# Attention, soft MoE and a squared-ReLU layer on one core: the start of the kernel rearranged around its branch

## The chip, the cores and the metric

The kernel runs as one program on one core of one Trainium2 chip. The metric is the device time of an execution in microseconds (us), and where several executions are given, their median. The engines are named as in the profile: PE is TensorE (PEld its weight loads), ACT is ScalarE, DVE is VectorE, POOL is GpSimd, SP is SyncE, which here only issues DMAs. A q behind an engine's name is its sequencer, which handles branches, waits and DMA issues.

## What is computed

Three layers in a row, all in float32. The sizes are 4 batches of 448 tokens, 12 heads of 64 (so 768 wide, and 24 pairs of heads over the batches).

```python
scores = matmul(q, k.T) / sqrt(64)
scores = cap * tanh(scores / cap)
attn = softmax(scores);  x = attn @ v                    # (4*448, 768)
logits = x @ phi                                         # phi: (768, 32)
d = softmax(logits, over tokens);  slot_input = d.T @ x  # 32 slots, 4 for each of 8 experts
slot_out[e] = relu(slot_input[e] @ w1[e]) @ w2[e]        # w1 (768, 1024), w2 (1024, 768)
x = softmax(logits, over slots) @ slot_out
h = relu(x @ w_in);  out = (h * h) @ w_out               # w_in (768, 2048), w_out (2048, 768)
```

## The kernel before

The order of all instructions is written out by hand (`manual_schedule`), so each engine executes its own instructions in the order of the code and waits on semaphores for the others.

*The start* (lines 76 to 245). SP requests `cap`. DVE makes `cabs` and `flag` of it; `flag` tells whether the cap is small enough for a softmax without its maximum. POOL meanwhile writes constants: one element of each ring buffer, the identity `ident`, `onesp` (for the sums of the softmax), `gcol`, `one1`, and then the selectors: `seld` and `selh` are sums of slices of `ident`, `ssum` and `selr` their copies spread over more columns. `ssum` sums over the four groups of tokens at the very end of attention (`last_end`), `selr` spreads the reciprocal sums of the last two pairs over the heads (`den_rows`, tile `bm`). Last, POOL clears `ktail` and `vtail`, which hold the last 64 rows of keys and values of a pair.

*Around the branch* (lines 576 to 586). SP requests the q and k of pairs 0 and 1 (`load`, tile `r`) and `phi` in four pieces. Then every engine reads `flag` into a register and branches for itself; there is no barrier. The block for a large flag stands first in the program, and the one that is executed here is reached by a jump. In it POOL requests the v of pair 0 (`load_v`, six pieces `va` and two `vtail`), DVE splits q and k into `hi` and `lo` (two parts whose products need one pass each), and SP requests pair 2 into the buffer of pair 0, for which it waits until `lo` has been made.

*A pair of heads* (`for i in range(NPAIR)`, 24 iterations). PE makes the scores in four groups of keys (`scores(i, g)`): three groups of 128 (line 323, two heads side by side) and the last 64 of both heads together (line 318, which reads `ktail`), each as three terms of `hi` and `lo`. There are two buffers for the scores, and ACT frees one with the tanh of a group (lines 327 and 325); ACT also makes the exponentials, two groups at a time (line 333). Between the groups of pair i, PE makes the products of pair i-1 with its v (`pv`, float32), the sums of its softmax (`den`, tile `dn`) and, from the fourth iteration on, the logits of pair i-3 with `phi_sb`. A float32 product is recorded twice, so six `pv` products are twelve records. DVE makes `hi` and `lo` of the next pair, and POOL fills `ktail` and requests v. SP's queue holds, in the order of the code, the q and k three pairs ahead, the spread of the reciprocal sums (`bc`), and the experts' weights.

*After attention* the experts run as fast as their weights come (lines 860 and 885), and then the last layer (lines 969 and 1089), where PE is never idle for long.

Of the kernel before, what the change touches and what calls it, by code (L numbers as in the profile page):

```python
# [8 lines left out]
F32 = mybir.dt.float32  # L9
# [10 lines left out]
P = 128  # L20
# [22 lines left out]
def softcap_attention_soft_moe_relu2(  # L43
# [75 lines left out]
    one1 = tmp.tile([1, 1], F32, name="one1")  # L119
    nc.gpsimd.memset(one1, 1.0)  # L120
    seld = tmp.tile([P, NS], F32, name="seld")
    add = lambda out, a, b: nc.gpsimd.tensor_tensor(out=out, in0=a, in1=b, op=ALU.add)
    ids = ident.rearrange("p (j s) -> p j s", j=4)
    add(seld, ids[:, 0], ids[:, 1])
    for j in (2, 3):
        add(seld, seld, ids[:, j])
    ssum = tmp.tile([P, 4, NS], F32, name="ssum")
    nc.gpsimd.tensor_copy(ssum, seld.unsqueeze(1).to_broadcast([P, 4, NS]))

    selh = tmp.tile([P, 2], F32, name="selh")  # L130
    idh = ident.rearrange("p (c h x) -> p c h x", c=4, h=2)[:, :, :, 0]
    add(selh, idh[:, 0], idh[:, 1])
    for c in (2, 3):
        add(selh, selh, idh[:, c])
    selr = tmp.tile([P, 2, D], F32, name="selr")
    nc.gpsimd.tensor_copy(selr, selh.unsqueeze(2).to_broadcast([P, 2, D]))
    phi_sb = tmp.tile([P, KD, NS], F32, name="phi_sb")


# [90 lines left out]
    with ExitStack() as att:  # L230
# [34 lines left out]
        def load(i):  # L265
            b, two, h = heads_of(i)
            t = raw_tile(i)
            nc.sync.dma_start(out=t, in_=qk[b, two, :, :, h].rearrange("j d r s -> (j d) r s"))
            st["raw", i] = t
# [59 lines left out]
        def exps(i, half):  # L329
            p = st["p", i, half].rearrange("p c h s -> p (c h s)")  # L330
            if half:
                p = p[:, :3 * S]
            nc.scalar.activation(p, p, AF.Exp, scale=cabs)  # L333
# [239 lines left out]
            if steps:  # L573
                steps.pop(0)()

        for i in range(2):
            load(i)
        for j in range(2):
            for h in range(2):
                nc.sync.dma_start(out=phi_sb[D * j:D * j + D, h::2], in_=phi[D * h:D * h + D, j::2])  # L580
        flag_v = nc.values_load(flag[:1, :1], min_val=0, max_val=1)
        with tc.If(flag_v == 0, preferred_fallthrough_block=False) as cond:
            load_v(0)
            prep_hi(0)
            prep_lo(0)
            load(2)
            for i in range(NPAIR):
                last = i == NPAIR - 1
                prv, old, tok = (i >= n for n in (1, 2, 3))
                scores(i, 0)  # L590
                scores(i, 1)
                exps(i, 0)
                if old:
                    take(i - 2)
                if tok:
                    norm(i - 3)
                if prv:
                    sums(i - 1, 1)
                if old:
                    den_rows(i - 2)  # L600
                if not last:
                    prep_hi(i + 1)
                    prep_lo(i + 1)
                if i + 3 < NPAIR:
                    load(i + 3)
                if prv:
                    for g in range(NG):
                        pv(i - 1, g)
                    den(i - 1, i - 3 if tok else None)
                if tok:  # L610
                    logits_add(i - 3)
                    if (i - 3) % HP == HP - 1:
                        late = batch_end((i - 3) // HP)
                        late.pop(0)()
                    elif (i - 3) % HP in (1, 2):
                        step()
                if i in range(4, 16, 2):
                    load_weight(NPAIR // 2 - 1 + (i - 4) // 4, part=i // 2 % 2)
                if i == NPAIR - 2:
                    load_weight(NB - 2, part=0)  # L620
                    load_weight(NB - 2, part=1)
                if (i, 2) in dsteps:
                    dsteps.pop((i, 2))()
                if i < 2 * len(early) and i % 2 == 0:
                    x = early[i // 2]
                    load_raw(*x, ring[NB - 1 - i // 2 % 2][:, :WSZ])
                    dsteps[i + 1, 1] = lambda x=x: decode_a(x)
                    dsteps[i + 2, 0] = lambda x=x: decode_b(x, nc.vector)
                    dsteps[i + 2, 1] = lambda x=x: decode_c([x], (0, 1))
                    dsteps[i + 3, 0] = lambda x=x: decode_c([x], (2,))  # L630
                    dsteps[i + 4, 2] = lambda x=x: store(x)
                if i % 2 and i < NPAIR - 1:
                    load_weight(i // 2)
                if (i, 0) in dsteps:
                    dsteps.pop((i, 0))()
                scores(i, 2)
                scores(i, 3)
                exps(i, 1)
                if prv:
                    pv(i - 1, NG)  # L640
                sums(i, 0)
                if tok:
                    to_tokens(i - 3)
                    if (i - 3) % HP == 0:
                        step()
                if not last:
                    load_v(i + 1)
                if i == 2:
                    load_weight(NB + 1)
                if i == NPAIR - 2:  # L650
                    load_weight(NB)
                    load_weight(NB - 3, part=0)
                    load_weight(NB - 3, part=1)
                if tok and (i - 3) % HP == HP - 1:
                    late.pop(0)()
                    steps.extend(late)
                if (i, 1) in dsteps:
                    dsteps.pop((i, 1))()
                if i == NPAIR - 4:
                    load_weight(NB - 1)  # L660
            assert not dsteps
            assert not steps
            n = NPAIR - 1
            pv(n, 0)
            pv(n, 1)
            sums(n, 1)
            den_rows(n - 1)
            load_weight(NB + 2, nc.scalar)
            pv(n, 2)
            pv(n, 3)  # L670
            norm(n - 2)
            norm(n - 1)
            den(n)
            to_tokens(n - 2, nc.scalar)
            logits(n - 2)
            den_rows(n)
            logits(n - 1, False)
            load_weight(NB + 3, nc.scalar)
            load_weight(NB + 4, nc.scalar)
            norm(n)  # L680
            to_tokens(n - 1, nc.scalar)
            logits(n, False)
            last_end(True)

        with cond.Else():
            st.clear()
            for n, x in enumerate(early):
                load_raw(*x, ring[NB - 1 - n % 2][:, :WSZ])
                decode_ab(x)
                decode_c([x])  # L690
                store(x)
# [487 lines left out]
```

## Time and profile before

| | us |
|---|---|
| median of 3 executions | 555.55 (555.1 to 557.49) |
| the profiled execution | 557.33 |
| its span, from the first to the last instruction | 555.5 |
| PE busy | 520.5 (94%) |
| DVE busy / ACT busy / POOL busy | 331.4 / 332.3 / 160.3 |
| PE on the chain that ended last | 78% |
| DMA on that chain | 12% |

By place: some 10 us pass before PE's first product; attention reaches to 212 us; the experts' weights set the pace to about 289 us; the last layer fills the rest. The profile also gives a granted TensorE clock for each stretch. It stands at 1.00 from the start, but nothing is recorded of it before 21 us, so there the clock is read from the distance between products: 448 columns need 0.37 us at 1.2 GHz and 0.19 us at 2.4 GHz.

In the rows below, times are in us from the start of the span, unless a number is marked as ns. "[1.70 <-PE sc L323]" behind an instruction says that its engine had been idle for 1.70 us and what ended that; "issue" stands where the profile shows nothing that the engine waited for. Records of matmuls overlap, since their ends are modelled, so the pace is read from their starts; x2 merges two records.

### The profile page before, as it was taken

What the parts mean: (1) busy time and instruction counts of PE and PEld (TensorE: products, weight loads), DVE (VectorE), ACT (ScalarE), POOL (GpSimd) and SP (SyncE); (2) the same over time, 40 slices, a digit from 0 to 9 for tenths busy, and PEclk for the clock granted to TensorE, in tenths of its full rate; (3) what the DMA queues carried; (4) which work ended last, traced back from release to release, by engine and by line L of the source; (5) the groups of instructions that cost most, each with busy time, mean ns of one, the idle gap of its engine ahead of it and who ended that gap; (6) DMA issues with size and microseconds to landing.
All of it is one profiled execution on the core that took longest, in us unless ns stands there. A gap on an engine that the chain in (4) does not pass through costs nothing.

```text
span 555.5 us, 10533 instructions
## 1 busy us (share of the span) xinstructions
PE 520.5 (94%) x4068; PEld 357.7 (64%) x4068; DVE 331.4 (60%) x529; ACT 332.3 (60%) x467; POOL 160.3 (29%) x347
## 2 busy tenths in 40 slices
PE   2999999999999989888679999999999999999997
PEld 1555556655655645444236888888888888788885
DVE  2499999999999765440018989889641231322111
ACT  2899999999899840000026677766654455633342
POOL 6987889788878601000000000000000000000000
PEclk9999999999999998999999999999999999999999
DMA  3688987899878799999998544551030110001002
GB/s 108 186 268 265 258 252 228 253 272 273 239 251 234 205 361 416 418 413 416 416 401 336 170 145 163 196 181 57 1 114 0 40 75 1 0 20 38 1 1 113
DMA packets 46249, 108.16 MB, mean 195 GB/s; under 512 B 19440, under 2 KB 28272, under 8 KB 46192
## 3 DMA queue, kind: packets, MB, share of 16 engines
q1 hardware_dynamic: 39472, 99.14, 50.9%
q0 software_dynamic: 6144, 5.52, 4.6%
q10 hardware_dynamic: 576, 2.75, 1.2%
q8 instruction: 34, 0.56, 0.4%
q14 instruction: 23, 0.19, 0.1%
HBM read 94.47 MB, written 7.86 MB: 184 GB/s over the span
## 4 chain that ended last, share of the span: by engine, by line
PE 78%; DMA 12%; ACT 3%; DVE 3%; issue 3%; SPq 0%; ACTq 0%; DVEq 0%
PE y L1089 35%; PE pv L355 9%; PE sc L323 8%; DMA rb<-in_w_dram 8%; PE y L1026 4%; DMA r<-in_w_dram 3%; PE dn L365 3%; PE sc L318 3%; PE pv L352 3%; PE h L969 2%; PE y L1030 2%; PE xm L419 1%; PE so L885 1%; ACT r L327 1%; PE u L490 1%
## 5 line engine op out<-in xcount | busy, mean ns | idle before, releaser
L1089 PE MATMUL y<-gh,wo 128*128 128x512 f32 x576 | 179.0, 393 | 0.4 <-ACT part L1036 0.4
L1089 PEld LDWEIGHTS y<-gh,wo 128*128 128x128 f32 x576 | 106.5, 188 | 24.2 <-issue 1.4
L1089 PE MATMUL y<-gl,wo 128*128 128x512 f32 x288 | 111.6, 390 | 0.0
L982 DVE TENSOR_TENSOR gl<-r,gh 128x512 fp32r<-128x512 f32 (+1 forms) x64 | 40.0, 625 | 112.7 <-ACT gh L981 110.8
L285 POOL DMA_DIRECT2D va<-in_v_dram x144 | 86.7, 609 | 2.5 <-issue 2.4
L973 ACT ACTIVATE r<-h 128x512 f32<-128x512 f32 (+1 forms) x64 | 34.8, 544 | 80.1 <-PE h L969 80.1
L327 ACT ACTIVATE r<-sc,tsc 128x896 f32<-128x896 f32 x72 | 69.5, 998 | 17.5 <-PE sc L323 17.4
L333 ACT ACTIVATE r<-r,cabs 128x1792 f32<-128x1792 f32 (+1 forms) x48 | 77.1, 1606 | 1.6
L1089 PEld LDWEIGHTS y<-gl,wo 128*128 128x128 f32 x288 | 54.1, 188 | 11.6
L355 PE MATMUL pv<-r,va 128*64 128x448 f32 x288 | 60.3, 553 | 0.0
L323 PE MATMUL sc<-hi 64*128 64x448 f32 x144 | 32.7, 449 | 10.9 <-DVE hi L294 10.1
L867 ACT ACTIVATE hs<-ph 128x256 f32<-128x256 f32 x8 | 3.1, 383 | 65.8 <-PE ph L860 65.8
L355 PEld LDWEIGHTS pv<-r,va 128*64 128x64 f32 x288 | 18.6, 138 | 29.9 <-issue 22.5
L980 ACT ACTIVATE r<-r 128x512 f32<-128x512 f32 (+1 forms) x62 | 35.8, 577 | 2.0
L981 ACT CAST gh<-r 128x512 fp32r<-128x512 f32 (+1 forms) x62 | 35.1, 566 | 2.0
L306 POOL CAST ktail<-hi 64x64 fp32r<-64x64 f32 x48 | 27.0, 562 | 22.6 <-DVE hi L294 20.8
L339 DVE SCALAR_TENSOR_TENSOR psum<-r,gcol 128x896 f32<-128x896 f32 x24 | 27.3, 1139 | 3.5 <-POOL ktail L306 3.5
L885 PE MATMUL so<-rb,ht 128*32 128x256 f32 x298 | 24.9, 382 | 4.2 <-DVE ht L873 2.1
L289 POOL DMA_DIRECT2D vtail<-in_v_dram x48 | 28.0, 587 | 2.2 <-issue 2.2
L300 DVE TENSOR_TENSOR lo<-r,hi 128x896 fp32r<-128x896 f32 x24 | 26.9, 1120 | 2.8 <-POOL ktail L306 0.5
L343 DVE TENSOR_TENSOR psum<-psum,r 128x896 f32<-128x896 f32 x24 | 26.0, 1085 | 4.1 <-ACT r L333 3.9
L873 DVE COPY ht<-px 128x32 f32<-128x32 f32 x8 | 1.5, 192 | 44.7 <-PE px L870 36.2
(195 smaller groups left out, 819.6 us busy)
## 6 DMA issues: line engine op xcount, KB each, us to landing
rb<-in_w_dram SPq DMA_DIRECT2D x41, 768.0 KB, 14.3
r<-in_qk_dram SPq DMA_DIRECT2D x24, 448.0 KB, 4.7
r<-in_w_out_dram SPq DMA_DIRECT2D x13, 768.0 KB, 4.3
r<-in_w_in_dram SPq DMA_DIRECT2D x9, 768.0 KB, 4.3
r<-in_w_dram SPq DMA_DIRECT2D x7, 896.0 KB, 17.2
rb<-in_w_in_dram SPq DMA_DIRECT2D x7, 768.0 KB, 6.8
bc<-rc SPq DMA_DIRECT2D x88, 56.0 KB, 4.1
rb<-in_w_dram SPq DMA_DIRECT2D x12, 384.0 KB, 5.2
```

Of the source, the lines that this page charges most:

```text
L285: nc.gpsimd.dma_start(out=va[r:r + n, g], in_=src[q:q + n, :, c])
L289: nc.gpsimd.dma_start(out=vt[rows, rows], in_=src[CP - D:, h, C - 1])
L323: nc.tensor.matmul(sc[:, h, :S], k, x[rows, 0], **flags)
L327: nc.scalar.activation(p, sc[:, :, :S], AF.Tanh, scale=tsc)
L333: nc.scalar.activation(p, p, AF.Exp, scale=cabs)
L355: nc.tensor.matmul(o[D * h:D * h + D, :S], va[:, g, h], p[:, h], start=(g == 0), stop=False,)
L885: nc.tensor.matmul(so[32 * j:32 * j + 32, :UNIT], ht[:, ft, :], weights(EU * e + EU // 2 + u), start=(e == 0 and ft == 0), stop=(e == NE - ...
L973: nc.scalar.activation(r[:, :n], h[:, :n], AF.Relu)
L980: nc.scalar.activation(r[:, :n], r[:, :n], AF.Square)
L981: nc.scalar.copy(gh[:, :n], r[:, :n])
L982: eng.tensor_tensor(out=gl[:, :n], in0=r[:, :n], in1=gh[:, :n].bitcast(F32), op=ALU.subtract)
L1089: nc.tensor.matmul(y[:, :nn], whl[ft][:, wi, ds], gx[:, :nn], start=(ft == first and t == 0), stop=(ft == end - 1 and t == 2),)
```

## The change

Four things move, and the work that the result needs stays the same.

- The eight POOL operations that build the selectors become a function that is called in the last iteration (and at the start of the other block).
- Of the q and k only pair 0 is requested ahead of the branch. Pair 1 follows as SP's first request behind it, and `phi` comes behind pair 2.
- `turn` makes extra products that nobody reads, into the buffers of `ps_m`: four of `ident` with itself ahead of the branch, four more as PE's first work behind it.
- In the first iteration eight more, of `hi` of pair 0 (128 x 448), behind the fourth group of scores.

```diff
-    add(seld, ids[:, 0], ids[:, 1])
-    for j in (2, 3):
-        add(seld, seld, ids[:, j])
...
+    def selectors():
+        add = lambda out, a, b: nc.gpsimd.tensor_tensor(out=out, in0=a, in1=b, op=ALU.add)
+        ids = ident.rearrange("p (j s) -> p j s", j=4)
+        add(seld, ids[:, 0], ids[:, 1])
...
+        nc.gpsimd.tensor_copy(selr, selh.unsqueeze(2).to_broadcast([P, 2, D]))
...
-        for i in range(2):
-            load(i)
-        for j in range(2):
-            for h in range(2):
-                nc.sync.dma_start(out=phi_sb[D * j:D * j + D, h::2], in_=phi[D * h:D * h + D, j::2])
+        load(0)
+
+        def load_phi():
+            for j in range(2):
+                for h in range(2):
+                    nc.sync.dma_start(out=phi_sb[D * j:D * j + D, h::2], in_=phi[D * h:D * h + D, j::2])
+
+        def turn(a, b, n):
+            t = ps_m.tile([P, 512], F32, tag="m", name="turn")
+            for _ in range(n):
+                nc.tensor.matmul(t[:a.shape[1], :b.shape[1]], a, b, start=True, stop=True)
+
+        turn(ident, ident, 4)
         flag_v = nc.values_load(flag[:1, :1], min_val=0, max_val=1)
         with tc.If(flag_v == 0, preferred_fallthrough_block=False) as cond:
+            turn(ident, ident, 4)
+            load(1)
             load_v(0)
             prep_hi(0)
             prep_lo(0)
             load(2)
+            load_phi()
             for i in range(NPAIR):
...
                 scores(i, 3)
+                if i == 0:
+                    turn(st["hi", 0][:, 0, :P], st["hi", 0][:, 0], 8)
                 exps(i, 1)
...
+                if last:
+                    selectors()
...
         with cond.Else():
             st.clear()
+            selectors()
+            load_phi()
```

Line numbers below are those of each kernel; the changed one's are 2 higher from the selectors on and 10 higher at the branch.

SP's queue up to the branch, before: two requests of `r` (pairs 0 and 1) and four of `phi_sb`, then the flag.

```order
L94 DMA capb<-in_cap_dram 128x1
L268 DMA r_75<-in_qk_dram 128x2x448 x2
L580 DMA phi_sb<-in_phi_dram 64x3x32 x4
L581 TENSOR_LOAD flag
L581 ISA x2
L582 COMPARE_AND_BRANCH
```

The same queue with the change.

```order
L94 DMA capb<-in_cap_dram 128x1
L270 DMA r_75<-in_qk_dram 128x2x448
L591 TENSOR_LOAD flag
L591 ISA x2
L592 COMPARE_AND_BRANCH
```

Five of the requests are gone from ahead of the branch. They are found again as SP's first rows in the block behind it, where the first row is pairs 1 and 2, and the third is pair 3:

```order
L270 DMA r_75<-in_qk_dram 128x2x448 x2
L583 DMA phi_sb<-in_phi_dram 64x3x32 x4
L270 DMA r_75<-in_qk_dram 128x2x448
L177 DMA rb_84<-in_w_in_dram 128x768
L270 DMA r_75<-in_qk_dram 128x2x448
```

There pairs 2 and 3 stood together before, directly ahead of the raw weights `rb_84`; now `phi` lies between them.

PE in the first pair, before: from its first product behind the branch to the first scores of pair 1 (`hi_271`).

```order
L323 MATMUL sc_0_254<-hi_245 128x448 x2
L323 MATMUL sc_0_254<-hi_245,lo_247 128x448 x2
L323 MATMUL sc_0_254<-lo_247,hi_245 128x448 x2
L323 MATMUL sc_1_262<-hi_245 128x448 x2
L323 MATMUL sc_1_262<-hi_245,lo_247 128x448 x2
L323 MATMUL sc_1_262<-lo_247,hi_245 128x448 x2
L323 MATMUL sc_2_281<-hi_245 128x448 x2
L323 MATMUL sc_2_281<-hi_245,lo_247 128x448 x2
L323 MATMUL sc_2_281<-lo_247,hi_245 128x448 x2
L318 MATMUL sc_3_289<-hi_245,ktail_189 128x448 x2
L318 MATMUL sc_3_289<-lo_247,ktail_189 128x448
L323 MATMUL sc_0_305<-hi_271 128x448 x2
```

The same with the change (the second and third group, which read alike, left out).

```order
L588 MATMUL turn<-ident 128x128 x4
L325 MATMUL sc_0_256<-hi_243 128x448 x2
L325 MATMUL sc_0_256<-hi_243,lo_245 128x448 x2
L325 MATMUL sc_0_256<-lo_245,hi_243 128x448 x2
...
L320 MATMUL sc_3_291<-hi_243,ktail_181 128x448 x2
L320 MATMUL sc_3_291<-lo_245,ktail_181 128x448
L588 MATMUL turn<-hi_243 128x448 x8
L325 MATMUL sc_0_316<-hi_273 128x448 x2
```

Four products now stand ahead of the first scores, and eight between the last scores of pair 0 and the first of pair 1; the order of the others is the same.

## Rows read from the trace of the kernel before

**Rows 1.** Chain of waits, 0 to 40 us: start, duration, what.
```profile
4.46 4.80 issue
...
9.99 1.10 DVE lo L300
...
12.46 1.97 ACT r L327 x2
```

**Rows 2.** Branch records (line 582): duration ns min/median/max, then start.
```profile
L582 PEldq COMPARE_BRANCH  x1: 4320/4320/4320, 4.3 to 4.3; - x1
...
L582 SPq COMPARE_BRANCH  x1: 45/45/45, 6.3 to 6.3; - x1
L582 POOLq COMPARE_BRANCH  x1: 45/45/45, 6.9 to 6.9; - x1
```

**Rows 3.** Line 268, the requests of q and k: SP's waits, and landing.
```profile
L268 SPq EVENT_SEMAPHORE  x22: 17/17/1097, 9.3 to 167.4; - x22
...
DMA to landing us min/median/max: 3.8/4.7/6.8
```

**Rows 4.** DMA queues, 4.2 to 6.1 us: packets, MB, share of 16 engines.
```profile
q1 hardware_dynamic: 881, 0.68, 105.6%
```

**Rows 5.** DMA queues, 6.1 to 6.4 us: those of instructions.
```profile
q8 instruction: 1, 0.02, 22.8%
q14 instruction: 2, 0.02, 12.9%
```

**Rows 6.** Timeline of POOL, 4 to 10 us: start, duration, instruction.
```profile
4.30 0.24 POOL L122 TENSOR_TENSOR seld<-ident 128x32 f32<-128x32 f32 x1
...
6.55 0.56 POOL L244 MEMSET ktail<- 128x256 f32 x2
...
9.82 0.90 POOL L285 DMA_DIRECT2D va<-in_v_dram  x1 [2.42 <-issue]
```

**Rows 7.** Timeline of SP, 0 to 14 us.
```profile
1.19 1.32 SPq L268 DMA_DIRECT2D r<-in_qk_dram  x2
2.56 2.56 SPq L580 DMA_DIRECT2D phi_sb<-in_phi_dram  x4
```

**Rows 8.** Timeline of PE, 10 to 25 us.
```profile
17.19 0.74 PE L323 MATMUL sc<-hi 64*128 64x448 f32 x2 [0.29 <-ACT r L327]
...
18.10 0.58 PE L323 MATMUL sc<-lo,hi 64*128 64x448 f32 x2
18.48 0.58 PE L323 MATMUL sc<-hi 64*128 64x448 f32 x2
...
19.73 3.12 PE L355 MATMUL pv<-r,va 128*64 128x448 f32 x12
...
23.80 0.36 PE L323 MATMUL sc<-hi,lo 64*128 64x448 f32 x2
24.00 0.36 PE L323 MATMUL sc<-lo,hi 64*128 64x448 f32 x2
```

**Rows 9.** Timeline of ACT, 10 to 60 us.
```profile
24.43 1.01 ACT L327 ACTIVATE r<-sc,tsc 128x896 f32<-128x896 f32 x1 [1.70 <-PE sc L323]
```

**Rows 10.** PE's timeline at 210 us; the stretch's busy times and granted clock (0.50).
```profile
210.66 1.54 PE L563 MATMUL m<-ident,u_sb 128*128 128x128 f32 x6
...
208.80:212.20 3.40, 3.38 (x46) 2.51 (x34) 2.66 (x6) 0.00 (x0) 1.36 (x3) 0.50 1.00 417
212.20:215.00 2.80, 2.79 (x48) 1.46 (x48) 0.96 (x3) 0.00 (x0) 0.00 (x0) 1.00 1.02 424
```

**Rows 11.** Waits of ACT and of PE, 24.4 to 195 us: total, times, longest.
```profile
ACT r L327 <- PE sc L323: 8.6, 11, 1.7
...
PE sc L323 <- ACT r L327: 0.4, 1, 0.4
```

**Rows 12.** Timelines near the end of attention: POOL's last v requests, PE's first `bm`.
```profile
189.68 1.06 POOL L289 DMA_DIRECT2D vtail<-in_v_dram  x2
...
198.45 0.49 PE L391 MATMUL bm<-rc,selr 32*128 32x112 f32 x8
```

More of the change, by code (lines that the diff above doesn't have):

```diff
@@ L121, in softcap_attention_soft_moe_relu2 @@
     seld = tmp.tile([P, NS], F32, name="seld")
-    add = lambda out, a, b: nc.gpsimd.tensor_tensor(out=out, in0=a, in1=b, op=ALU.add)
-    ids = ident.rearrange("p (j s) -> p j s", j=4)
-    add(seld, ids[:, 0], ids[:, 1])
-    for j in (2, 3):
-        add(seld, seld, ids[:, j])
     ssum = tmp.tile([P, 4, NS], F32, name="ssum")
-    nc.gpsimd.tensor_copy(ssum, seld.unsqueeze(1).to_broadcast([P, 4, NS]))
     selh = tmp.tile([P, 2], F32, name="selh")
[L131 to L134, printed above, removed]
     selr = tmp.tile([P, 2, D], F32, name="selr")
-    nc.gpsimd.tensor_copy(selr, selh.unsqueeze(2).to_broadcast([P, 2, D]))
+    def selectors():
+        add = lambda out, a, b: nc.gpsimd.tensor_tensor(out=out, in0=a, in1=b, op=ALU.add)
+        ids = ident.rearrange("p (j s) -> p j s", j=4)
+        add(seld, ids[:, 0], ids[:, 1])
+        for j in (2, 3):
+            add(seld, seld, ids[:, j])
+        nc.gpsimd.tensor_copy(ssum, seld.unsqueeze(1).to_broadcast([P, 4, NS]))
+        idh = ident.rearrange("p (c h x) -> p c h x", c=4, h=2)[:, :, :, 0]
+        add(selh, idh[:, 0], idh[:, 1])
+        for c in (2, 3):
+            add(selh, selh, idh[:, c])
+        nc.gpsimd.tensor_copy(selr, selh.unsqueeze(2).to_broadcast([P, 2, D]))
     phi_sb = tmp.tile([P, KD, NS], F32, name="phi_sb")
```

## The prediction

> **What bounds the kernel now.** I read the chain of waits first, for the first 40 us. Its largest link there is no work at all: DVE has taken the branch at 4.46 and then stands in "issue" for 4.80 us until 9.25, does `hi` and `lo` of pair 0, and ACT's first tanh starts at 12.46 [rows 1]. So 12 us pass before the first tanh, and the change works on exactly this stretch.
>
> Why DVE stands there: not for its data, since pair 0's request at 1.19 [rows 7] takes 4.7 us to land in the median [rows 3]. The branch records and the DMA view tell more. PE branches at 4.3 and needs 4.32 us for it, to 8.6; SP branches at 6.3 and acts again at 9.3, POOL at 6.9 and acts at 9.82 [rows 2, 3, 6]. The late branches take 2.9 to 3.0 us, the early ones 4.3 to 4.8. From 4.2 to 6.1 the data queue fills the DMA engines (105.6% of their time) and no packet of the instruction queues moves [rows 4]; from 6.1 to 6.4 three of them move at once [rows 5]. So the jump needs code, and the code of the three early engines waited for pair 1 and `phi`, which SP had requested from 1.19 to 5.12 [rows 7].
>
> Next I read PE in the first pairs. The products of pair 1 start 0.37 us apart (18.10, 18.48), which is 448 columns at 1.2 GHz; after 23.80 they start 0.20 us apart, which is 2.4 GHz [rows 8]. PE had run without a pause from 17.19 and changed pace inside the pv block of 19.73. At the low level it makes ACT wait once, 1.70 us before the tanh at 24.43 [rows 9].
>
> After that PE is the pace: from 24.4 to 195 us ACT waits for PE 8.6 us in all (1.7 of it the wait just named) and PE for ACT 0.4 us [rows 11]. A microsecond that PE gains by 24.4 is therefore kept through attention. Behind it lies a stretch that the weights' DMAs set, but SP issues these in the order of the same loop, so they are requested earlier by as much. I count the shift one to one to the end.
>
> **The change, part by part.**
>
> *Selectors.* Eight POOL operations leave the start, from 4.30 to the memset at 6.55: 2.25 us [rows 6]. POOL then branches at about 4.65 instead of 6.9 and, with the same 2.9 us, issues the first v request at about 7.6 instead of 9.82. This is not on the chain by itself. In the last iteration they stand behind the last v request, which ends at 190.74, and their first reader on PE is at 198.45 [rows 12]: 7.7 us of cover for 2.25 us. The reload instruction that now stands ahead of them has no price in a row; the cover would hide up to 5.4 us of it. Zero.
>
> *Requests behind the branch.* SP loses one qk request and four phi requests ahead of the branch, some 3.2 us of issue [rows 7], and so branches with the others, at about 4.7. In the branch come pair 1, pair 2 (which waits for `lo` of pair 0) and then phi, whose 2.56 us push pair 3 back; that one is read two pairs later. Zero. Phi's first reader is pair 0's logits in the fourth iteration. Pair 1, requested at about 7.7, lands at 11.5 to 14.5 (3.8 to 6.8 us [rows 3]); with 1.8 us of `hi` and `lo` it is there by 16.3 at worst, and its scores are due at about 15.9, so 0 to 0.4 us; I take 0.
>
> *The branch itself.* With only pair 0 ahead, the code of DVE has free queues. Bounds: 4.8 us as now, 2.9 as POOL's. I take 2.95, nearer to the late branches because the cause of the difference is what is removed: DVE acts at 7.4 and has `lo` at 9.25 (1.84 us as in rows 1). PE's block is the larger one (one q8 packet has as many bytes as two of q14 [rows 5]), so I take 3.4 us of 2.9 to 4.32: PE acts at 7.7.
>
> *Four products after the branch.* Each is two records, as in the pv row, where six products give twelve [rows 8]. The nearest row for their price is the transposes of 128 columns in a stretch granted 0.50: six in 1.54 us, 0.257 each [rows 10]. Eight records make 2.05 us, from 7.7 to 9.75. At 2.4 GHz they would be half of that. So it is PE, not DVE, that is late: three terms of 0.37 follow, then the last one's tail (0.58 - 0.37 [rows 8]) and the hand-over, and ACT starts at about 11.15 instead of 12.46: **1.3 us** won. Without these products DVE's `lo` would give 10.6. Bounds: 10.4 (PE at 7.0) to 12.05 (PE at 8.6 as now): 2.05 to 0.4 us. The four ahead of the branch need `ident` and run while PE has nothing to do; zero.
>
> *Eight products in pair 0.* They come behind the fourth score group, where PE has a pause of 0.29 us at present, ahead of 17.19, until ACT frees a buffer [rows 8]. Here ACT starts 1.3 us sooner and POOL delivers `ktail` 2.25 us sooner, so I see the group end at about 14.4 if the clock rises ahead of it, at 14.7 if not, and pair 1's scores due at 15.9 (17.19 - 1.3). At 0.20 us apiece the eight take 1.6 us, to 16.0: almost all in the pause. At 0.37 us they take 3.0 us, to 17.7.
>
> *The clock.* From 7.7 on PE now goes on nearly without a pause to 16, where before it had pauses from 10 to 17. The stretch 208.8 to 212.2 had the same sort of work, small products and then 128-column transposes, ran at 0.50, and PE's clock was up behind it [rows 10]. So I take it that PE is at 2.4 GHz before the eight products. Then scores, pv and the sums of pair 0 are at full pace: from 16.0 two score groups (6 x 0.20 and a tail, 1.45), pv (12 x 0.20, 2.4), the sums (0.7, as from the pv's end at 22.85 to the scores near 23.5) and one group (0.85), 5.4 us to 21.4; and ACT, free at 22.73 before (24.43 - 1.70), is free at 21.4 [rows 8, 9]. The gap of **1.7 us** closes.
>
> The Trainium skill, page "TensorE: Matmul & The Clock Gate", section "What's actually happening", speaks against counting on this: the number of products at the low level differs between runs of one kernel, and the ramp is under 1% of a typical span and should not be fitted to. The trace agrees on the size (1.70 us of 555.5). By it the clock part is a matter of luck, which is the second rival below.
>
> *Sum.* 1.3 + 1.7 = 3.0 us. The profiled execution took 557.33 (span 555.5 and 1.83 around it); it would take 554.3. The median of the runs is 555.55, so the forecast is 552.6.
>
> **Rivals.**
>
> *The code comes no faster.* For: PE's 4.32 may be its larger block and not the queue. Against: no instruction packet moved before 6.1 [rows 4]. Then PE acts at 8.6, ACT starts at 12.05, and only the clock part is won: 0.4 + 1.7 = 2.1, **553.4**. The Trainium skill's page "Runtime: NRT & Kernel Launch", section "Instruction fetch mechanics", says that a taken branch out of the loaded window waits for a DMA of its target; that the length follows the other requests stands only in the rows.
>
> *The clock rises late.* The eight products run at 1.2 GHz and push pair 1's scores from 15.9 to 17.7. Even if all is at 2.4 GHz from there, the tanh that is at 24.43 now comes at 17.7 + 5.4 = 23.1: 1.3 us won; if pv still starts slow, about 0.8. Between the two, 1.1: **554.4**. For: PE's work ahead of 17.19 did not raise the clock either, and the products of 18.10 and 18.48 still ran at the low level [rows 8].
>
> *Slower.* All five engines now branch between 4.3 and 4.9, where two of them came 2 us later. If their code is delivered one after another and PE's last, PE loses about what those two came later (2.0 and 2.6 us [rows 2]) and acts at 9.9 instead of 7.7; behind it stand the 2.05 us of products, so ACT starts at 13.3; with the clock late as well, the tanh of 24.43 comes at 25.25, 0.8 us later: **556.4**. It decides from PE acting later than about 9.1. Against: three packets moved together within 0.3 us [rows 5].
>
> **How the numbers follow.** Forecast 0.55, no faster code 0.15, late clock 0.20, slower 0.08, and 0.02 for a larger loss that I don't see. The forecast's own bounds are 551.8 (ACT at 10.4) to 553.5. Executions of the old kernel in which the clock rose later than in the profiled one (there may be some: the runs lie from 555.1 to 557.49) would add up to half a microsecond to the gain, so the low end is 551.2. The high end is 555.0, past the late clock; the slower case is left out. Half a per cent is 2.8 us, about what a measurement of this kernel can tell from no change; the forecast's 3.0 is just beyond. Of its 0.55 some 0.4 fall below 552.8, and of the others, with pair 1's clock better or worse than assumed, 0.08: faster 0.48, same 0.48, slower 0.04.
>
> **What would show it.** The branch: PE's branch record near 3.4 us and DVE's first `hi` near 7.4; at 8.6 and 9.3 the first step is wrong. The products: ACT's first tanh at 11.2, with PE busy without a pause ahead of it. The clock: products of pair 0's third or fourth group 0.20 us apart, and no ACT wait in pair 1; if the eight products stand 0.37 us apart, the second step is wrong. The selectors: PE's `bm` products must not wait for POOL. The prediction fails outright if the whole shift at pair 2 is not found again at the end.

## The result and the profile after

The change makes the kernel slower. The changed kernel takes 559.69 us in the median of 20 executions (557.15 to 561.88), the kernel before 556.88 beside it (555.0 to 568.41); the ratio is 1.0062, with a 95% interval of 1.0046 to 1.0077. Now and then an execution of these kernels lies some 8 us above the others; the ratios leave those out, which for the kernel with `ktail` first and all the products leaves three of six executions and then two of twelve.

The profiled execution took 558.41 us (span 556.6), 1.1 us more than the one before; the medians are 2.8 us apart. The start, which the change is about, did get shorter. The branches, as in [rows 2]; the number ahead of "to" is the start:

```profile
L592 PEldq COMPARE_BRANCH  x1: 3836/3836/3836, 4.3 to 4.3; - x1
...
L592 SPq COMPARE_BRANCH  x1: 45/45/45, 4.5 to 4.5; - x1
L592 POOLq COMPARE_BRANCH  x1: 45/45/45, 4.8 to 4.8; - x1
```

PE's timeline of the first pair, as in [rows 8]:

```profile
8.20 2.07 PE L588 MATMUL turn<-ident 128*128 128x128 f32 x8 [3.97 <-issue]
10.20 0.74 PE L325 MATMUL sc<-hi 64*128 64x448 f32 x2
...
14.90 1.04 PE L320 MATMUL sc<-hi,ktail 128*128 128x448 f32 x2 [0.74 <-POOL ktail L308]
...
15.98 1.78 PE L588 MATMUL turn<-hi 128*128 128x448 f32 x8
17.69 0.47 PE L325 MATMUL sc<-hi 64*128 64x448 f32 x2
```

And ACT's, as in [rows 1, 9]:

```profile
11.87 1.99 ACT L329 ACTIVATE r<-sc,tsc 128x896 f32<-128x896 f32 x2 [8.14 <-PE sc L325]
...
23.18 1.01 ACT L329 ACTIVATE r<-sc,tsc 128x896 f32<-128x896 f32 x1 [0.77 <-PE sc L325]
```

The first tanh comes 0.59 us sooner (12.46 before), that of pair 1's third group 1.25 us sooner (24.43), and attention keeps this: its last tanh is at 194.66 instead of 195.83. (How much of the 1.25 us is the change's own is taken up below: the kernel before does not always come as late as 24.43.) Then it is lost. The last link of DMA in the chain of waits, before and after:

```profile
274.82 13.22 DMA rb<-in_w_dram
```

```profile
275.69 13.38 DMA rb<-in_w_dram
```

These weights land at 288.04 before and at 289.07 after, and from there to the end of the span it is 267.5 us in both (555.5 - 288.04, 556.6 - 289.07). So between these two executions the whole loss lies from the end of attention to the last expert weights: 1.2 us ahead became 1.0 us behind. The stretches of 195 to 220 us (busy time of the engines, granted clock, DMA share, GB/s), before and after:

```profile
195.00:204.00 9.00, 8.55 (x87) 4.39 (x86) 5.47 (x9) 4.64 (x8) 0.00 (x0) 1.00 0.98 364
204.00:212.00 8.00, 6.35 (x75) 4.36 (x73) 5.44 (x21) 1.92 (x6) 1.36 (x3) 0.80 0.94 379
212.00:216.00 4.00, 3.44 (x52) 1.76 (x51) 1.11 (x4) 0.38 (x1) 0.00 (x0) 0.97 1.01 421
216.00:220.00 4.00, 3.75 (x50) 1.95 (x50) 2.03 (x8) 0.31 (x1) 0.00 (x0) 1.00 1.02 410
```

```profile
195.00:204.00 9.00, 8.03 (x92) 3.85 (x90) 4.96 (x8) 4.06 (x8) 0.00 (x0) 1.00 0.93 336
204.00:212.00 8.00, 6.25 (x79) 4.01 (x80) 5.78 (x22) 1.34 (x5) 1.32 (x3) 0.77 0.96 353
212.00:216.00 4.00, 3.83 (x44) 1.61 (x36) 0.04 (x1) 0.04 (x1) 0.00 (x0) 0.61 0.82 272
216.00:220.00 4.00, 3.36 (x42) 1.93 (x45) 2.03 (x8) 0.66 (x2) 0.00 (x0) 1.00 0.99 386
```

Read the last column: 28, 26, 149 and 24 GB/s less, over 9, 8, 4 and 4 us, are 1.15 MB that were not moved, 2.8 us at the 416 GB/s of the stretch behind. Two things could have done that. The clock column is lower too (0.61 instead of 0.97 in the third line), so PE might free the buffers later. Or the requests came late. They did; SP's first four requests of `rw`, before and after:

```profile
196.63 0.37 SPq L166 DMA_DIRECT2D rw<-in_w_dram  x1
201.65 0.33 SPq L166 DMA_DIRECT2D rw<-in_w_dram  x1
202.03 0.42 SPq L166 DMA_DIRECT2D rw<-in_w_dram  x1
202.50 0.75 SPq L166 DMA_DIRECT2D rw<-in_w_dram  x1
```

```profile
199.69 0.33 SPq L168 DMA_DIRECT2D rw<-in_w_dram  x1
203.26 0.33 SPq L168 DMA_DIRECT2D rw<-in_w_dram  x1
211.37 0.33 SPq L168 DMA_DIRECT2D rw<-in_w_dram  x1
213.79 0.33 SPq L168 DMA_DIRECT2D rw<-in_w_dram  x1
```

And what they wait for is found on another engine's queue. ACT requests three weights near the end of attention (lines 668 to 679 before, 685 to 696 after). Two of them, after, each with its start and the time from request to landing:

```profile
L168 ACTq DMA_DIRECT2D r<-in_w_dram x1: 334/334/334, 202.3 to 202.3; - x1
...
DMA to landing us min/median/max: 9.0/9.0/9.0
...
L168 ACTq DMA_DIRECT2D r<-in_w_dram x1: 389/389/389, 202.7 to 202.7; - x1
...
DMA to landing us min/median/max: 11.0/11.0/11.0
```

202.3 + 9.0 and 202.7 + 11.0 are 211.3 and 213.7: SP's third and fourth request leave within 0.1 us of these landings (the second leaves 0.1 us behind the landing of ACT's first, requested at 197.97; the first leaves as SP's own last weight lands, requested at 195.57 and 4.1 us on its way). SP's waits from 195 to 215 us name these transfers too. The longest of them (total, times, longest), before and after:

```profile
SPq L166 <- PE u L490: 6.0, 1, 6.0
```

```profile
SPq L168 <- DMA r<-in_w_dram: 12.9, 3, 7.8
```

Before, there is no wait for `r` among them, and the data do not ask for one: `rw` and `r` are different buffers.

The programs' instruction lists do ask for it. Each request made by SP or ACT signals one of eight semaphores, taken in turn, and waits until the request that had this semaphore before has landed. The turn is handed out in the order of the code in kernel.py, not of execution. The block for a large flag is the second one there (though it stands first in the program); both blocks begin at the count that the branch had, and the requests behind both go on from the count of the second. Pair 1's request has moved from ahead of the branch into the executed block, and the other block, which asks for pairs in its own way, has no such request (`phi`, which has moved too, is requested in both). So the other block's count is one lower, and behind the blocks the turn starts with 5 where it started with 1. (By its count the kernel before would have gone on with 6; 6, 7 and 0 are held by ACT's three requests, and the first request skips to 1. Starting with 5 nothing is skipped, and the next ones fall on 6, 7 and 0.) The semaphores of the five requests, in the two kernels and in four that are run below:

```
request       before  changed  changed+1  before+4  before+6  before+7
rw, first        1       5         1          2         4         5
rw, second       2       6         2          3         5         6
rw, third        3       7         3          4         6         7
rw, fourth       4       0         4          5         7         0
rx               5       1         5          6         0         1
ACT's three: 6, 7 and 0 in each; SP's last one ahead of them: 5
```

### The profile page after: what moved, and what is told of

Read it like the earlier page. It is cut to its first block, busy times and chain, and to the rows that moved or that the text cites. A ratio compares the mean times of both kernels' runs of the same rounds, so it can differ in the third digit from the quotient of the medians.

```text
span 556.6 us, 10582 instructions
## 1 busy us (share of the span) xinstructions
PE 525.3 (94%) x4092; PEld 362.0 (65%) x4092; DVE 331.3 (60%) x529; ACT 332.4 (60%) x467; POOL 160.4 (29%) x347
## 4 chain that ended last, share of the span: by engine, by line
PE 78%; DMA 11%; ACT 3%; issue 2%; DVE 2%; POOL 1%; SPq 0%; POOLq 0%; ACTq 0%; DVEq 0%
PE y L1108 35%; PE pv L357 9%; PE sc L325 8%; DMA rb<-in_w_dram 8%; PE y L1045 4%; PE sc L320 3%; DMA r<-in_w_dram 3%; PE dn L367 3%; PE pv L354 3%; PE h L988 2%; PE y L1049 2%; PE so L904 2%; PE xm L421 1%; PE ph L879 1%; ACT r L329 1%
## 5 line engine op out<-in xcount | busy, mean ns | idle before, releaser
L1108 PEld LDWEIGHTS y<-gl,wo 128*128 128x128 f32 x288 | 54.1, 188 | 11.6
L357 PEld LDWEIGHTS pv<-r,va 128*64 128x64 f32 x288 | 18.4, 136 | 29.1 <-issue 21.8
L308 POOL CAST ktail<-hi 64x64 fp32r<-64x64 f32 x48 | 27.2, 567 | 22.7 <-DVE hi L296 20.9
```

The source lines that it names most:

```text
L357: nc.tensor.matmul(o[D * h:D * h + D, :S], va[:, g, h], p[:, h], start=(g == 0), stop=False,)
L1108: nc.tensor.matmul(y[:, :nn], whl[ft][:, wi, ds], gx[:, :nn], start=(ft == first and t == 0), stop=(ft == end - 1 and t == 2),)
```

## The experiments

**The turn, given back and taken away.** Theory R says that the turn alone costs the time, rival C that it is the lower clock, rival S the selectors. Only code that is never executed is changed. In the changed kernel, one more DMA in the other block:

```diff
             selectors()
             load_phi()
+            nc.sync.dma_start(out=phi_sb[:D, ::2], in_=phi[:D, ::2])
```

> The changed kernel with one more DMA (a quarter of phi) in the block for a large flag, which is not executed here. The order of the eight DMA semaphores that the requests behind the two blocks go through starts with 1 again, as in the kernel before, and not with 5. Theory R (rotation): the requests of rw leave SP within some 7 us of 195.5 again and not at 199.7, 203.3, 211.4 and 213.8; the start's gain of some 1.2 us is then found at the end: ratio to the kernel before about 0.998 (0.9965 to 0.9995). Rival C (clock: the extra products of the start make the low level near 210 last 6.8 us instead of 3.4) and rival S (selectors built late): the loss stays, ratio 1.005 to 1.008.

Measured: 0.9976 (0.995 to 1.0003), median 555.76 beside 555.86. The loss is gone, and rival S with it, since the selectors are still late. Its `rw` requests and two of its stretches:

```profile
197.45 6.69 SPq L168 DMA_DIRECT2D rw<-in_w_dram  x4
```

```profile
204.00:212.00 8.00, 5.66 (x75) 3.73 (x73) 5.35 (x21) 1.92 (x6) 1.32 (x3) 0.85 1.00 408
212.00:216.00 4.00, 3.99 (x37) 1.78 (x40) 1.10 (x4) 0.00 (x0) 0.00 (x0) 0.50 1.01 414
```

The four leave within 6.7 us again (14.4 in the changed kernel), and the queue stays full. The second stretch also answers rival C: the clock is at its low level throughout (0.50, lower than the changed kernel's 0.61), and nothing is lost. Whether the start's gain arrives this run can't say: its interval touches 1, and in its profile neither pair 1's third group (24.59; why, below) nor the end of attention (last tanh at 195.84) is earlier than before. Its span is 1.5 us shorter all the same, as the queue moved more than before from 195 to 212 us (397 and 408 GB/s, where it had been 364 and 379); what makes that difference is not shown.

The reverse, in the kernel before: n DMAs that are never executed, seven of them and as a control four:

```diff
             st.clear()
+            for q in range(n):
+                j, h = q // 2 % 2, q % 2
+                nc.sync.dma_start(out=phi_sb[D * j:D * j + D, h::2], in_=phi[D * h:D * h + D, j::2])
```

> The kernel before with seven more DMAs in the block that is not executed; behind the blocks the semaphores then start with 5, as in the changed kernel. What is executed is the kernel before, instruction by instruction. Theory R: the second, third and fourth rw request leave SP when the three weights of ACT's queue land (about 205, 213 and 217 in the trace of the kernel before, earlier if they have the queue for themselves), and the time is up by what the change lost plus what its start had won: ratio 1.006 to 1.011. Rivals C and S: nothing of theirs is in it, ratio 1.000 (0.998 to 1.002).

> Control for the run with seven: the kernel before with four more DMAs in the block that is not executed; the semaphores behind the blocks start with 2. Theory R: requests one to four go through semaphores 2 to 5, whose transfers have landed by 200.6, and rx through 6 (205.4, and it leaves at 210.7 anyway), so the ratio is 1.000 (0.998 to 1.002). If requests that are never made cost something by themselves, for instance by the place of the code, this one is slower too, by 4/7 of the run with seven.

Measured: seven 1.0074 (1.0046 to 1.0102), four 1.0009 (0.998 to 1.0038). With seven, the trace has the pattern of the changed kernel, though every executed instruction is that of the kernel before:

```profile
199.83 0.33 SPq L166 DMA_DIRECT2D rw<-in_w_dram  x1
203.39 0.33 SPq L166 DMA_DIRECT2D rw<-in_w_dram  x1
212.09 0.33 SPq L166 DMA_DIRECT2D rw<-in_w_dram  x1
214.27 0.33 SPq L166 DMA_DIRECT2D rw<-in_w_dram  x1
```

Six of them lie between, with the turn starting at 4.

> The kernel before with six more DMAs in the block that is not executed; the semaphores behind the blocks then start with 4. Between the run with four (start 2) and the one with seven (start 5). Theory R: the third rw request waits for the first weight of ACT's queue (about 205), the fourth for the second (about 212), rx for the third (about 215); the first two leave as before. So fewer bytes are late than with seven, and the ratio lies between: 1.003 to 1.006. If it is the number of DMAs in the other block and not the order of the semaphores, 6/7 of the loss with seven and no break between four and six: 1.006.

Measured: 1.0035 (1.000 to 1.007), median 559.55 beside 556.29. Now it is the third and fourth that wait for ACT's first and second weight, which land at 206.2 and 210.1 (198.4 + 7.8, 202.7 + 7.4):

```profile
206.21 0.33 SPq L166 DMA_DIRECT2D rw<-in_w_dram  x1
...
210.13 0.33 SPq L166 DMA_DIRECT2D rw<-in_w_dram  x1
```

So the size of the loss follows which requests share a semaphore with ACT's weights. A loss by the number of DMAs that are never executed would be the rival, and the control alone leaves room for it: four sevenths of the 0.46 to 1.02% of seven are 0.26 to 0.58%, and its interval reaches 0.38%. Against it stand the run with one more, in which such a DMA takes the loss away, and the waits: from 195 to 215 us SP waits for `r` 13.2 us with seven and 12.2 us with six, and not at all with the one more in the changed kernel.

**The start without its products.** As the changed kernel with one more DMA, and without the calls of `turn`:

```diff
-        turn(ident, ident, 4)
...
-            turn(ident, ident, 4)
...
-                if i == 0:
-                    turn(st["hi", 0][:, 0, :P], st["hi", 0][:, 0], 8)
```

> As the changed kernel with one more DMA in the block that is not executed, and with all three calls of turn left out (4, 4 and 8 extra products). What is left of the change is the selectors and the requests behind the branch. If the products are worth what the prediction said, ACT's first tanh is not later than 11.9 (DVE's lo sets it), the clock rises near 20 us as in the kernel before, ACT waits about 1.5 us in pair 1, and the ratio to the kernel before is 0.9985 to 0.9995. Rival: the products buy nothing, and the ratio is that of the run with them, about 0.998.

Measured: 0.9993 (0.9978 to 1.0008). The first tanh is at 11.79, 0.1 us sooner than with the products, pair 1's third group at 23.76 after 1.30 us of waiting for PE. The products' worth, 0.9993 against 0.9976, is inside the intervals.

**The parts alone.** Each is one part of the change made in the kernel before, with the turn starting at 1.

```diff
-        for i in range(2):
-            load(i)
+        load(0)
...
+            load(1)
             load_v(0)
             prep_hi(0)
             prep_lo(0)
             load(2)
+            load_phi()
```

> The kernel before with one part of the change: pair 1 and phi are requested behind the branch. Selectors stay at the start, there are no extra products, and one DMA more in the block that is not executed keeps the semaphores behind the blocks starting with 1. POOL so branches at 6.9 as before, the four others between 4.3 and 4.6. Theory Q (the code waited for the data queue only from the branch to 6.1, some 0.7 us of the 4.8): DVE acts at 8.4 to 8.8 and PE at 7.8 to 8.2, as in the changed kernel, and the ratio is 0.998 to 0.9995. Rival F (five blocks of code at once hold each other up): with POOL's 2.5 us later DVE acts at 7.4 to 8.0, ratio 0.996 to 0.998.

> The kernel before with the selectors alone moved to the last iteration; requests, products and the semaphores behind the blocks are as before. Theory: POOL branches at 4.8 and issues v about 1 us sooner, nobody on the chain waits for that, and DVE still acts at 9.2 to 9.4: ratio 1.000 (0.998 to 1.002). Rival S (selectors in the last iteration hold up POOL or its readers): up to 2 us late near 198 us, ratio 1.002 to 1.005. Rival F: POOL's code moves together with that of PE, DVE and ACT from 6.1 on, and PE acts at 9.0 or later instead of 8.6.

Measured: requests 0.9988 (0.9955 to 1.0021), selectors 0.9979 (0.9949 to 1.0009); neither can be told from no change. With the requests alone DVE's `hi` starts at 8.30 and PE acts at 8.15 (4.29 + 3.86), close to theory Q. POOL, which branches at 6.87 there, acts at 9.80, after 2.93 us, while PE and DVE, with ACT's and SP's jumps beside them, take 3.9. With the selectors alone POOL branches at 4.83 and still acts only at 9.87: the 2 us went into a jump of 5.04 us, while SP's data still filled the queue.

**No jump at the start.** The executed block is put first in the program, so that the branch falls through and every engine jumps at the block's end:

```diff
-        with tc.If(flag_v == 0, preferred_fallthrough_block=False) as cond:
+        with tc.If(flag_v == 0, preferred_fallthrough_block=True) as cond:
```

> The kernel before with the other block second in the program, so that the executed block follows the branch and no engine jumps at the start; every engine jumps at the end of the block instead. Theory J (the wait of 4.8 us is the jump's code): DVE's first hi starts when pair 0 has landed, at 5.9 to 6.5, ACT's first tanh at 9 to 9.7, and attention ends some 2.5 to 3 us sooner. At its end each engine pays 3 to 4 us: SP between rb and the first rw (near 193), PE behind attention (near 208). If the weights in flight cover this, ratio 0.994 to 0.997; if SP's jump leaves the queue dry, 0.998 to 1.004. Rival: DVE waits for something else than code, and hi still starts near 9.3.

Measured: 1.0078 (1.0045 to 1.0111). The start is what theory J says, DVE's first `hi` and ACT's first tanh and fourth:

```profile
5.48 0.63 DVE L294 CAST hi<-r 128x896 fp32r<-128x896 f32 x1 [1.46 <-DMA r<-in_qk_dram]
```

```profile
8.61 1.96 ACT L327 ACTIVATE r<-sc,tsc 128x896 f32<-128x896 f32 x2 [4.85 <-PE sc L323]
...
16.89 0.63 ACT L325 ACTIVATE r<-sc,tsc 128x448 f32<-128x448 f32 x1 [3.60 <-PE sc L318]
```

3.85 us are won at the first tanh, and 0.15 are left at the fourth (17.04 before), where PE waits for `ktail`: POOL is as late as ever, being busy with the selectors and the clearing of its tiles until 9.8. The end was mis-sized; I had 3 to 4 us for its jump:

```profile
L582 PEldq COMPARE_BRANCH  x2: 90/3142/6193, 4.3 to 210.9; - x2
```

```profile
212.00:216.00 4.00, 0.00 (x0) 0.00 (x0) 0.38 (x1) 0.00 (x0) 0.00 (x0) 0.50 1.04 413
216.00:220.00 4.00, 2.75 (x23) 1.13 (x24) 0.49 (x2) 0.00 (x0) 0.00 (x0) 0.50 0.22 83
```

PE's jump took 6.19 us there, behind a full data queue; PE freed no weight buffer meanwhile, SP made no request from 210.64 to 219.21, and the queue ran dry (0.22).

**`ktail` first.** In the changed kernel PE waits 0.74 us for `ktail` (in the run with one more DMA 1.21). POOL fills it behind eight requests of v; now ahead of them, without and with the products:

```diff
-            load_v(0)
             prep_hi(0)
             prep_lo(0)
+            load_v(0)
```

> The kernel of the run without products (requests behind the branch, selectors late, semaphores starting with 1), and POOL now fills ktail of pair 0 ahead of its eight requests of v instead of behind them. The fourth group of pair 0, which waits for ktail until 15.3 there, comes when ACT frees a buffer, near 13.8; ACT's fourth tanh moves from 16.76 to 16.4 at best, since ACT is busy until then. v lands some 1.3 us later, by 19, just when its products start. Theory P (from pair 1 on PE is the pace, so the clock decides and not ktail): 0.3 us at most, ratio to the kernel before 0.998 to 1.000, like the run without products. Rival: ktail's wait is passed on to the end whole, ratio 0.996 to 0.998.

> As the changed kernel with one more DMA in the block that is not executed, and ktail of pair 0 ahead of v on POOL. The 1.2 us in which PE waits for ktail ahead of the fourth group, behind which the clock had fallen again there, close. Theory K (a pause of PE there lets the clock fall, and then the eight products run 0.37 us apart): the clock rises between 11.5 and 14 and stays, the eight products stand 0.20 us apart, tanh of pair 1's third group comes at 21.5 to 23.2, and the ratio to the kernel before is 0.995 to 0.998. Rival L (when the clock rises is a matter of the execution): it may rise at 18 or later all the same, and the ratio is that of the run with one more DMA, 0.997 to 0.9995.

Measured: without the products 0.9987 (0.9936 to 1.0037), with them 0.9947 (0.9893 to 1.0001). With the products PE has no pause, the eight run at 2.4 GHz, and ACT's gap in pair 1 closes (no bracket behind the tanh):

```profile
14.70 1.79 PE L588 MATMUL turn<-hi 128*128 128x448 f32 x8
16.64 0.47 PE L325 MATMUL sc<-hi 64*128 64x448 f32 x2 [0.16 <-ACT r L329]
```

```profile
22.12 1.01 ACT L329 ACTIVATE r<-sc,tsc 128x896 f32<-128x896 f32 x1
```

Against this the run with one more DMA, where PE paused for `ktail` and the clock, already up, fell back:

```profile
15.05 1.31 PE L320 MATMUL sc<-hi,ktail 128*128 128x448 f32 x2 [1.21 <-POOL ktail L308]
...
16.53 2.64 PE L588 MATMUL turn<-hi 128*128 128x448 f32 x8
19.10 0.47 PE L325 MATMUL sc<-hi 64*128 64x448 f32 x2
```

The same kernel again, and one with only the eight products left:

```diff
-        turn(ident, ident, 4)
...
-            turn(ident, ident, 4)
```

> The same kernel as in the run tail first with products, for a narrower interval and a second look at the clock. Theory K: the clock rises between 11 and 14.5 us and stays up, the eight products stand 0.20 us apart, tanh of pair 1's third group comes near 22.1, ratio 0.996 to 0.998. Rival L (when the clock rises is a matter of the execution): it rises at 17 or later here, the eight stand 0.37 us apart, tanh at 24 or later, ratio 0.998 to 1.000.

> As the run tail first with products, without the four products ahead of the branch and the four behind it; only the eight behind the fourth group of pair 0 are left. Theory (the earlier products are what raises the clock): the clock rises later than 16, the eight run 0.37 us apart and push pair 1 back, tanh of its third group at 23.5 to 25, ratio 0.998 to 1.000. Rival (the unbroken score groups raise it): rises by 14.5 as with all sixteen, tanh near 22.1, ratio 0.995 to 0.998.

Measured: again 1.0042 (0.9992 to 1.0093), median 564.56; the eight alone **0.9977 (0.9965 to 0.9988)**, median 554.81 beside 556.08. The clock rose early in both, at 13.2 and 15.1 us, as theory K and the second run's rival had it, so with the eight alone the products around the branch were not needed for it. The eight then stand 0.21 us apart (15.20 + 1.81) and the tanh comes at 22.41. That kernel beats the kernel before by 0.23%, and the changed one: it has the selectors late, the requests behind the branch, one more DMA in the other block, `ktail` first and eight products. Its trace ends attention 2.0 us ahead of the profiled kernel before (last tanh at 193.80), which fits a gain of the start. But its ratio does not stand out from that of the selectors alone (0.9979, 0.9949 to 1.0009), so which part brings how much the times do not tell.

The repeated kernel shows something else. Its start is the best of all (tanh at 21.87), and at the end of attention its trace is 7 us later than that of the first run (last tanh at 201.98 and 194.88). POOL's work from 40 to 190 us (the last number ahead of the second bar is the mean in ns), in the first run:

```profile
L308 POOL CAST ktail<-hi 64x64 fp32r<-64x64 f32 x38 | 22.4, 589 | 17.1 <-DVE hi L296 15.6
L308 POOL CAST ktail<-lo 64x64 fp32r<-64x64 f32 x39 | 10.6, 272 | 3.3 <-DVE lo L302 1.0
```

and in the repeat:

```profile
L308 POOL CAST ktail<-lo 64x64 fp32r<-64x64 f32 x37 | 31.8, 860 | 2.2
L308 POOL CAST ktail<-hi 64x64 fp32r<-64x64 f32 x36 | 31.4, 871 | 1.9
```

In the first POOL waits for DVE; in the repeat it waits for nobody, and its casts of `hi` take one and a half times as long, those of `lo` three times. I read this as casts that now fall on DVE operations. The Trainium skill, page "SBUF — State Buffer", section "SBUF: two separate sides", says that DVE in some of its modes and GpSimd share a pair of ports, and whichever instruction starts first holds it to its end. The traces agree in kind (casts of 0.23 us when alone, about 1 us beside DVE's work); which DVE operation holds the ports was not tried. A milder case is the run with four more DMAs, which executes the instructions of the kernel before: its casts take 792 and 522 ns, where those of the kernel before take 609 and 232, and its last tanh is at 199.96 instead of 195.83. What decides into which rhythm an execution falls stays open. Of the fourteen traces only these two show it, and both are among the three in which ACT does not wait ahead of pair 1's third group (the third is the first run of this kernel); that is too little to call it the cause.

## Why the prediction was wrong, step by step

**The step that failed** stands in the last two sentences of "What bounds the kernel now": that SP issues the weights "in the order of the same loop, so they are requested earlier by as much", and the shift is counted one to one to the end. The order is the same, and ACT's last tanh is indeed 1.17 us sooner in the changed kernel's trace. But a request also waits for its semaphore, and the turn of the semaphores had moved by the change. Its price is 0.74% alone (seven more DMAs in the kernel before) and is the difference between 0.9976 and 1.0062 in the changed kernel, about 4 to 5 us. None of the rivals had it; they all looked at the first 25 us. The prediction priced what a moved request costs ahead of and behind the branch, and not what the other block's count of requests does behind both. A count from the last weights on would have held: from the landing of the last request of the expert weights to the end of the span it is 266.7 to 267.2 us in all fourteen traces.

**The start was a gain, and mis-sized.** Forecast 3.0 us at pair 1's third group, measured 1.25 between the two profiled executions, and that number is in part luck. In four executions of the instructions of the kernel before (its own and those with four, six and seven more DMAs) this tanh starts at 24.43, 22.70, 23.74 and 23.53; in two of the changed kernel's (its own and the one with one more DMA) at 23.18 and 24.59. What stays put is the first tanh, 12.40 to 12.49 and 11.87 to 11.89: 0.5 to 0.6 us won, of 1.3 forecast.

- *That the wait is the jump's code* was right: without the jump DVE acts at 5.48.
- *The price of the jump* was wrong. I took 2.95 us for DVE and 3.4 for PE from the late branches; they were 4.0 (4.41 to 8.42) and 3.84. Empty queues saved only 0.5 to 0.9 us of 4.3 to 4.8. PE acted at 8.14, half way between my 7.7 and the 8.6 of the rival that the code comes no faster. (My low bound, PE at 7.0, was below even what 2.9 us allow, 7.2.) What I had not seen is that a late branch is cheap because it is late: with the requests alone POOL, which branches 2.5 us behind the others, takes 2.93 us, and four or five engines that branch together take 3.5 to 4.4. That it is the number of engines that makes this difference is my reading of these rows; it was not tried by itself. The rival of a strict queue, one engine after another (PE at 9.9), is excluded by the same rows.
- *The four products* cost 2.07 us (2.05 forecast), and next to nothing of it counts: PE's scores start at 10.20, and DVE's `lo`, which they need from the second term on, ended at 10.25. Without the products the first tanh is 0.1 us sooner.
- *The eight products and the clock* came as forecast in the changed kernel's profile, 0.20 us apart, but pair 1's scores started at 17.69 and not at 16.0, since `ktail` was late by 0.74 us and the first tanh by 0.7. With `ktail` first they start at 16.64, and the tanh is at 22.1 against my 21.4.
- *The clock's 1.7 us* were sized by one execution, and the trace that I had was the one with the longest wait. In the other three of the four executions named above ACT waits 0, 0.70 and 0.47 us ahead of this tanh, with no product added.
- *Whether the clock is up in time* is not settled by the products alone. In the run with one more DMA it was up at 11.6, down again at 15.0 behind PE's wait for `ktail`, and most of the eight ran at 1.2 GHz (it was up again at 18.4): the second rival's 17.7 for pair 1's scores, there 19.1. The rule I cited from the Trainium skill ("TensorE: Matmul & The Clock Gate", "What's actually happening"), that the ramp differs between runs, holds here: in nine traces whose first pair lacks the eight products the clock is first recorded at its high level anywhere from 14.7 to 22.7 us, and in the four among them that execute the same instructions from 14.7 to 21.1. With `ktail` first and the eight it was 13.2, 13.2 and 15.1.
- *The selectors* at zero: nothing speaks against it (alone 0.9979, 0.9949 to 1.0009). In the changed kernel POOL builds them from 189.75 to 192.2, and PE reads them at 197.30.

What would be seen was partly named: "fails outright if the whole shift at pair 2 is not found again at the end". It is there at the end of attention and not at the end.

## What to carry to other kernels

Where a program hands out DMA semaphores in turn, a request that is moved, added or left out anywhere ahead in the code, even in a block that is not executed, can change which later requests wait for which transfers. After such an edit compare the semaphores of the requests that keep a full queue full, and look in the trace for requests that leave at the very moment at which an unrelated transfer lands. And where a late stage is set by transfers, a shift won early has to be followed to the requests of that stage, not only to the engines that issue them.

## What the runs showed of the hardware that I had not expected

- From a taken branch to the engine's next work it is 2.9 us for POOL when it branches 2.5 us behind the others, 3.5 to 4.4 for four or five engines at once, 4.2 to 5.0 behind SP's requests at the start, 6.19 for PE behind a full weight queue. Without the jump DVE starts as soon as its data is there, at 5.48.
- Small POOL casts of 0.23 us take about 1 us beside DVE's work, and a chain of them can stay in that rhythm through most of attention: mean 871 and 860 ns instead of 589 and 272 in the same kernel, with attention 7 us longer.
- The low level of TensorE's clock for four whole microseconds (212 to 216, granted 0.50) took nothing from the stream of the weights: 414 GB/s there, and 408 and 416 beside it, in the run with one more DMA.
